# Batch 0's loads moved to another queue, and the copies of batches 0 and 1 reordered over ScalarE and VectorE

## The chip, the cores and the metric

The kernel runs on one core of one Trainium2 chip. A core has a matrix engine (TensorE, PE in the profile, its weight loads PEld), a vector engine (VectorE, DVE), an activation engine (ScalarE, ACT), GpSimd (POOL) and a queue engine (SyncE, SP). Each works through its own instructions in order, and they wait for each other by semaphores. Transfers are issued from SP's, ACT's or POOL's queue and share 16 DMA engines. The metric is device microseconds of one execution; the median of several executions is compared.

## What is computed

An efficient attention per batch and head, and a gated feed-forward block on its result, in float32 at the interfaces:

```python
# q, k, v: (8, 8, 576, 64)
q_s = softmax(q, axis=-1)            # over the 64 features
k_s = softmax(k, axis=2)             # over the 576 positions
kv = einsum('bhsd,bhse->bhde', k_s, v)
x = einsum('bhsd,bhde->bhse', q_s, kv)   # -> (4608 tokens, 512)
out = (silu(x @ w_gate) * (x @ w_val)) @ w_out   # 512 -> 1536 -> 512
```

## The kernel before, in words

**Attention.** Each batch is handled in two groups G of four heads. A load brings q, k or v of a group as a tile of 128 partitions x 1152 float32 (576 KB). ACT takes exponentials (`exp_of`, line 124: eq, ek). VectorE sums eq over the features, takes the reciprocal (`norm_sum`, lines 138 and 143: rs, rr) and multiplies (`norm_mul`, line 152: qs). TensorE transposes qs in nine 128x128 pieces into two banks of PSUM, of five and four pieces (`turn_pe`, line 166: tp), and they are copied to qt (`turn_out`, lines 111 and 113). TensorE multiplies ek with v (kv), which is scaled by one over the sum of ek into kn. Then kn times qt gives xp (`x_one`, line 221), and ACT (line 228) and VectorE (line 229) each copy one half of it into xt, the feed-forward's input. PSUM has eight banks here, handed out in program order as they come free.

**Feed-forward.** `m_unit` (line 278) does one of twelve slices m of the hidden width: four gate matmuls and four value matmuls per piece of tokens (line 289: g_ps, u_ps), a silu on ACT (line 297) and a product on VectorE into hr (line 298). Batch 0's 576 tokens are two pieces of 320 and 256. `o_mm` (line 314) makes 128 output tokens in twelve matmuls, `o_out` copies them on VectorE (line 322) and stores them from SP. `o_last` (line 328) does the final 128 tokens in two halves of 256 columns.

**Order.** The order of each engine's instructions is the order of the program text (`tc.manual_schedule`). Batch 0 comes first and is written out by hand: its q and k loads for both groups and its v loads (cast to bfloat16 on the way, v16) are POOL DMAs (lines 344 to 350), followed in POOL's queue by the making of the identity, half of one multiply (line 368) and 14 weight loads (lines 372 to 375). Its key sums come from small matmuls (`key_sum`, line 385: ks, kvr), its kv from `kv_first` (line 396) and its scaling from `scale_first` (line 409: one half on ACT, one on VectorE). `spin` (line 377) issues matmuls on zeros that nobody reads; they keep TensorE busy. Then come the twelve slices of batch 0, while SP loads batches 1 and 2. These loads wait until the second of four w_out loads has landed (line 440). Next is a stage that interleaves batch 1's attention (`kv_one`, `scale_one`) with output units 0 to 3 (lines 446 to 475), after which ACT takes batch 2's exponentials. From line 477 on, chunks of 512 tokens (the first of 448) run with the attention of the next batch between their slices.

Of the kernel before, what the change touches and what calls it, by code (L numbers as in the profile page):

```python
# [15 lines left out]
def kernel(  # L16
# [10 lines left out]
    nc = tc.nc  # L27
# [19 lines left out]
    def bank(name):  # L47
        return psp.tile([128, 512], FP32, tag="ps", name=name)
# [16 lines left out]
    def head_ap(src, b, G, t0=0, t1=T):  # L65
        return bass.AP(
            tensor=src.tensor,
            offset=src[b, 4 * G].offset + 64 * t0,
            ap=[[T * 64, 128], [2 * HSTR, 2], [1, (t1 - t0) * 64]],
        )  # L70
# [48 lines left out]
    def exp_of(what, b, G, pieces=((0, T),)):  # L119
        s = st.setdefault((b, G), {})  # L120
        e = s["e" + what] = at.tile([128, T, 2, 64], BF16, tag="e" + what, name="e" + what)
        src = raw[what, b, G].rearrange("p h (t d) -> p t h d", d=64)
        for t0, t1 in pieces:
            nc.scalar.activation(out=e[:, t0:t1], in_=src[:, t0:t1], func=AF.Exp)  # L124
# [7 lines left out]
    def norm_sum(b, G, pieces=((0, T),)):  # L132
        s = st[b, G]
        eq2 = s["eq"].rearrange("p t h d -> p (t h) d")
        rs = at.tile([128, 2 * T], FP32, tag="rs", name="rs")
        first = None
        for t0, t1 in pieces:
            i = nc.vector.reduce_sum(  # L138
                out=rs[:, 2 * t0:2 * t1], in_=eq2[:, 2 * t0:2 * t1, :], axis=mybir.AxisListType.X
            )  # L140
            first = first or i
        rr = s["rr"] = at.tile([128, 2 * T], FP32, tag="rr", name="rr")
        nc.vector.reciprocal(out=rr, in_=rs)
        return first

    def norm_mul(b, G, pieces=((0, T),), engs=None):
        s = st[b, G]
        eq2 = s["eq"].rearrange("p t h d -> p (t h) d")
        qs = s["qs"] = at.tile([128, T, 128], BF16, tag="qs", name="qs")
        for (t0, t1), eng in zip(pieces, engs or (nc.vector, nc.vector)):  # L150
            n = 2 * (t1 - t0)
            eng.tensor_mul(  # L152
                qs[:, t0:t1, :].rearrange("p t (h d) -> p (t h) d", d=64),
                eq2[:, 2 * t0:2 * t1, :],
                s["rr"][:, 2 * t0:2 * t1].to_broadcast([128, n, 64]),
            )
# [13 lines left out]
    def turn_out(b, G, i, eng):  # L170
        s = st[b, G]
        t0, t1 = BANKS[i]
        copy(
            eng,
            s["qt"][:, t0:t1, :],
            s["tp", i][:, 0:(t1 - t0) * 128].rearrange("p (t c) -> p t c", c=128),
        )
# [23 lines left out]
    def scale_one(b, G, engs):  # L201
        s = st[b, G]
        kn = s["kn"] = at.tile([128, 2, 128], BF16, tag="kn1", name="kn1")
        for g in range(2):
# [5 lines left out]
            else:  # L210
                nc.vector.tensor_scalar_mul(kn[:, g, :], kv[:, 0:128], kvr)

    def x_one(b, G):
        s = st.pop((b, G))
        for t0, t1 in BANKS:
            n = 64 * (t1 - t0)
            xp = [bank("xp") for _ in range(2)]
            for g in range(2):
                for h in range(2):
                    r = slice(64 * h, 64 * h + 64)  # L220
                    nc.tensor.matmul(  # L221
                        out=xp[h][64 * g:64 * g + 64, 0:n],
                        lhsT=s["kn"][r, g, r],
                        rhs=s["qt"][r, t0:t1, 64 * g:64 * g + 64],
                        start=True, stop=True,
                    )
            c0 = b * S + 64 * t0
            nc.scalar.copy(out=xt[:, 2 * G, c0:c0 + n], in_=xp[0][:, 0:n])  # L228
            nc.vector.tensor_copy(out=xt[:, 2 * G + 1, c0:c0 + n], in_=xp[1][:, 0:n])

# [45 lines left out]
    def m_unit(c0, n, m, by_part=False):  # L278
        ms = slice(m * 128, (m + 1) * 128)
        parts = [(c0, n)] if n <= 512 else [(c0, 320), (c0 + 320, n - 320)]  # L280
        gu = []
        for w, nm in ((wg, "g_ps"), (wv, "u_ps")):
            ps = [bank(nm) for _ in parts]
            steps = [(kk, i) for kk in range(KT) for i in range(len(parts))]
            if by_part:
                steps.sort(key=lambda a: (a[1], a[0]))
            for kk, i in steps:
                c, w_ = parts[i]
                nc.tensor.matmul(  # L289
                    out=ps[i][:, 0:w_], lhsT=w[:, kk, ms], rhs=xt[:, kk, c:c + w_],  # L290
                    start=(kk == 0), stop=(kk == KT - 1),
                )
            gu.append(ps)
        for g_ps, u_ps, (c, w_) in zip(gu[0], gu[1], parts):
            r = c % RING
            sg = ff.tile([128, 512], BF16, tag="sg", name="sg")
            nc.scalar.activation(out=sg[:, 0:w_], in_=g_ps[:, 0:w_], func=AF.Silu)  # L297
            nc.vector.tensor_mul(hr[:, m, r:r + w_], sg[:, 0:w_], u_ps[:, 0:w_])  # L298
# [18 lines left out]
            )  # L317
        return o_ps

    def o_out(j, o_ps):  # L320
        o_sb = osb.tile([128, 512], FP32, tag="o_sb", name="o_sb")
        nc.vector.tensor_copy(out=o_sb, in_=o_ps)  # L322
        store(j, o_sb)

    def o_unit(j):
        o_out(j, o_mm(j))

    def o_last(j):
        r0 = (j * 128) % RING
        o_sb = osb.tile([128, 512], FP32, tag="o_sb", name="o_sb")  # L330
        for c0 in (0, 256):
            o_ps = bank("o_ps")
            for m in range(MT):
                nc.tensor.matmul(  # L334
                    out=o_ps[:, 0:256], lhsT=hr[:, m, r0:r0 + 128], rhs=wo[:, m, c0:c0 + 256],
                    start=(m == 0), stop=(m == MT - 1),
                )
            nc.vector.tensor_copy(out=o_sb[:, c0:c0 + 256], in_=o_ps[:, 0:256])
            store(j, o_sb, c0, c0 + 256, (nc.sync, nc.scalar))

    with tc.manual_schedule():
        for what, src in (("q", q), ("k", k)):
            for G in range(NG):
                t_ = raw[what, 0, G] = ld.tile([128, 2, T * 64], FP32, tag=what, name=what)
                nc.gpsimd.dma_start(out=t_, in_=head_ap(src, 0, G))
        nc.gpsimd.dma_start(out=v16[0], in_=head_ap(v, 0, 0))
        for t0, t1 in BANKS:
            nc.gpsimd.dma_start(out=v16[1][:, :, 64 * t0:64 * t1], in_=head_ap(v, 0, 1, t0, t1))  # L350

# [6 lines left out]
            nc.vector.memset(sel[64 * g:64 * g + 64, g:g + 1], 1.0)  # L358
        for vb in vbs:
            nc.vector.memset(vb[:, :, 128:129], 1.0)  # L360
        make_identity(nc, ident)

        exp_of("q", 0, 0, BANKS)
        exp_of("q", 0, 1)
        exp_of("k", 0, 0)

        first = norm_sum(0, 0, BANKS)
        norm_mul(0, 0, BANKS, (nc.vector, nc.gpsimd))
        norm_sum(0, 1)
        norm_mul(0, 1, BANKS)  # L370

        for c0, n in ((0, 128), (128, 256), (384, 384), (768, 384), (1152, 384)):
            w_slice(wg, moe_w_gate, c0, n)
# [32 lines left out]
                        start=(t == 0), stop=(t == T - 1),  # L406
                    )

        def scale_first(G):
            s = st[0, G]  # L410
            kn = s["kn"] = at.tile([128, 2, 128], BF16, tag="kn1", name="kn1")
            nc.scalar.mul(kn[:, 0, :], s["kv"][0][:, 0:128], s["kvr"][:, 0:1])
            nc.vector.tensor_scalar_mul(kn[:, 1, :], s["kv"][1][:, 0:128], s["kvr"][:, 1:2])

        spin(8)
        spin(6, first)
        turn_pe(0, 0, 0)
        turn_pe(0, 0, 1)
        turn_out(0, 0, 0, nc.scalar)
        turn_out(0, 0, 1, nc.scalar)  # L420
        exp_of("k", 0, 1)
        key_sum(0)
        spin(3)
        turn_pe(0, 1, 0)
        turn_pe(0, 1, 1)
        turn_out(0, 1, 0, nc.scalar)
        turn_out(0, 1, 1, nc.vector)
        key_sum(1)
        spin(2)
        kv_first(0)  # L430
        scale_first(0)
        spin(2)
        x_one(0, 0)
        kv_first(1, *BANKS[0])
        kv_first(1, *BANKS[1])
        scale_first(1)
        spin(2)
        x_one(0, 1)

        load_batch(1, w_dma[-3], by_group=True)  # L440
        load_batch(2)
# [1 line left out]
        for m in range(MT):  # L443
            m_unit(0, S, m, by_part=(m == 0))

        for G in range(NG):
            exp_of("q", 1, G)
            exp_of("k", 1, G)
            cast_v(1, G)
        norm_sum(1, 0)  # L450
        norm_mul(1, 0)
        o_unit(0)
        o_unit(1)
        turn_pe(1, 0, 0)
        turn_pe(1, 0, 1)
        turn_out(1, 0, 0, nc.vector)
        turn_out(1, 0, 1, nc.vector)
        kv_one(1, 0)
        norm_sum(1, 1)
        scale_one(1, 0, (nc.vector, nc.vector))  # L460
        norm_mul(1, 1)
        p = o_mm(2)
        x_one(1, 0)
        turn_pe(1, 1, 0)
        turn_pe(1, 1, 1)
        o_out(2, p)
        turn_out(1, 1, 0, nc.vector)
        turn_out(1, 1, 1, nc.vector)
        kv_one(1, 1)
        scale_one(1, 1, (nc.vector, nc.vector))  # L470
        o_unit(3)
        x_one(1, 1)
        for what in ("q", "k"):
            for G in range(NG):
                exp_of(what, 2, G)

        chunks = [(S, 448)] + [(c, 512) for c in range(1024, n_tok, 512)]
        for ci, (c0, n) in enumerate(chunks):
# [85 lines left out]
```

## Time and profile before

| | us |
|---|---|
| median of 8 runs | 322.92 (321.64 to 324.13) |
| profiled execution, its own time | 323.65 |
| profiled execution, span from first to last instruction | 321.9 |
| TensorE busy | 310.8 (97%) |
| first gate matmul of batch 0 starts | 19.14 |
| first output matmul starts | 42.86 |
| first gate matmul of the chunk loop starts | 58.30 |
| last copy of an output starts | 317.84 |

The page gives busy time and clock by engine, and the groups of instructions. The timeline gives for each instruction or run of like instructions its start, its duration, engine, line, operation, output and inputs, and in brackets how long the engine sat idle before it and what ended that. Durations of matmuls are of pipelined instructions, so a run of them counts by its whole length. A DMA issue is listed with its queue, size and the time from issue to landing.

### The profile page before, as it was taken

The numbers are of one execution on the slowest core, as the hardware profiler recorded it, in microseconds if no ns is written. First come the engines' busy times: TensorE is split into PE (matmuls) and PEld (weight loads), VectorE is DVE, ScalarE is ACT, GpSimd is POOL, SyncE is SP. The second block draws the span as 40 slices with busy tenths as digits, with TensorE's granted clock in tenths as the row PEclk, the third lists the DMA queues.
The fourth block names the chain that finished last, engine by engine and source line by source line (L and its number), as shares of the span: only waits on it lengthen the run. The fifth ranks groups of instructions, "written<-read, shape, count | busy, mean of one in ns | idle before, by whom it ended". The sixth has DMA issues, their size and how long they took to land.

```text
span 321.9 us, 4888 instructions
## 1 busy us (share of the span) xinstructions
PE 310.8 (97%) x1897; PEld 153.3 (48%) x1897; DVE 164.9 (51%) x281; ACT 143.9 (45%) x209; POOL 34.1 (11%) x42
## 2 busy tenths in 40 slices
PE   5899998999999999999999999999999999999994
PEld 1468754455444444454444444444444444444443
DVE  2544459298493639363935484457545233333421
ACT  3663381744637454735574467346734122312200
POOL 7950011200200020002000200020000000000000
PEclk9799999999999999999999999999999999999999
DMA  6999999327653934584438533862420112020124
GB/s 191 239 202 204 229 397 390 118 39 230 249 114 67 336 130 103 71 305 169 102 69 266 210 77 72 241 259 56 82 67 0 35 32 65 0 63 4 34 67 100
DMA packets 39848, 45.75 MB, mean 142 GB/s; under 512 B 17424, under 2 KB 24080, under 8 KB 39824
## 3 DMA queue, kind: packets, MB, share of 16 engines
q1 hardware_dynamic: 31392, 37.63, 39.8%
q0 software_dynamic: 8272, 7.67, 13.2%
q8 instruction: 15, 0.25, 0.3%
q10 hardware_dynamic: 160, 0.13, 0.2%
q14 instruction: 9, 0.07, 0.1%
HBM read 37.75 MB, written 9.44 MB: 147 GB/s over the span
## 4 chain that ended last, share of the span: by engine, by line
PE 85%; DMA 6%; ACT 3%; DVE 3%; issue 1%; POOL 0%; ACTq 0%; POOLq 0%
PE g_ps L289 28%; PE u_ps L289 27%; PE o_ps L314 25%; DMA q<-in_q_dram 4%; PE kv L191 2%; DMA out_dram<-o_sb 2%; ACT eq L124 1%; DVE rs L138 1%; PE xp L259 1%; DVE qs L152 1%; PE o_ps L334 1%; PE idle L380 1%; ACT ek L124 1%; DVE hr L298 1%; PE kv L403 1%
## 5 line engine op out<-in xcount | busy, mean ns | idle before, releaser
L297 ACT ACTIVATE sg<-g_ps 128x512 bf16<-128x512 f32 (+2 forms) x120 | 64.9, 554 | 137.3 <-PE g_ps L289 131.8
L298 DVE TENSOR_TENSOR hr<-sg,u_ps 128x512 bf16<-128x512 bf16 (+2 forms) x120 | 74.4, 630 | 89.1 <-PE u_ps L289 80.4
L289 PE MATMUL g_ps<-xt,wg 128*128 128x512 bf16 (+2 forms) x480 | 111.6, 358 | 0.3 <-ACT xt L228 0.2
L289 PE MATMUL u_ps<-xt,wv 128*128 128x512 bf16 (+2 forms) x480 | 111.0, 358 | 0.0
L314 PE MATMUL o_ps<-wo,hr 128*128 128x512 bf16 x420 | 93.6, 379 | 0.0
L289 PEld LDWEIGHTS <-wv 128*128 128x128 bf16 x480 | 46.9, 98 | 46.7 <-issue 0.4
L289 PEld LDWEIGHTS <-wg 128*128 128x128 bf16 x480 | 45.8, 98 | 45.4 <-issue 1.4
L314 PEld LDWEIGHTS <-hr 128*128 128x128 bf16 x420 | 40.9, 98 | 49.1
L322 DVE COPY o_sb<-o_ps 128x512 f32<-128x512 f32 x35 | 23.7, 681 | 40.3 <-PE o_ps L314 40.3
L127 POOL CAST vb<-v 128x1152 bf16<-128x1152 f32 x14 | 16.1, 1148 | 178.0 <-DMA v<-in_v_dram 151.2
L138 DVE TENSOR_REDUCE rs<-eq 128x18 f32<-128x1152 bf16 (+2 forms) x17 | 21.6, 1277 | 14.5 <-ACT eq L124 14.5
L152 DVE TENSOR_TENSOR qs<-eq,rr 128x1152 bf16<-128x1152 bf16 (+2 forms) x17 | 21.1, 1246 | 0.2
L124 ACT ACTIVATE eq<-q 128x1152 bf16<-128x1152 f32 (+2 forms) x17 | 18.0, 1101 | 5.6 <-DMA q<-in_q_dram 5.6
L124 ACT ACTIVATE ek<-k 128x1152 bf16<-128x1152 f32 x16 | 17.9, 1157 | 0.4 <-DMA k<-in_k_dram 0.3
L297 ACT ACT_TABLE_LOAD x12 | 15.4, 1283 | 0.2
L124 ACT ACT_TABLE_LOAD x11 | 14.1, 1283 | 0.2
L380 PE MATMUL idle<-zero 128*128 128x512 bf16 x23 | 9.0, 534 | 3.8 <-DVE rs L138 2.5
L191 PE MATMUL kv<-vb,ek 64*128 64x129 bf16 x252 | 8.9, 217 | 0.2 <-DVE hr L298 0.2
L191 PEld LDWEIGHTS <-ek 64*128 64x128 bf16 x252 | 7.4, 94 | 3.0 <-ACT sg L297 2.1
L267 ACT CAST xt<-xp 128x512 bf16<-128x512 f32 x12 | 6.4, 589 | 3.8 <-PE xp L259 3.8
L268 DVE CAST xt<-xp 128x512 bf16<-128x512 f32 x12 | 7.7, 682 | 0.0
L228 ACT CAST xt<-xp 128x320 bf16<-128x320 f32 (+1 forms) x8 | 2.8, 402 | 10.6 <-PE xp L221 10.6
(48 smaller groups left out, 74.8 us busy)
## 6 DMA issues: line engine op xcount, KB each, us to landing
out_dram<-o_sb SPq DMA_DIRECT2D x70, 128.0 KB, 2.4
q<-in_q_dram SPq DMA_DIRECT2D x14, 576.0 KB, 5.1
k<-in_k_dram SPq DMA_DIRECT2D x14, 576.0 KB, 7.4
v<-in_v_dram SPq DMA_DIRECT2D x14, 576.0 KB, 9.2
wo<-in_moe_w_out_dram POOLq DMA_DIRECT2D x4, 384.0 KB, 16.2
q<-in_q_dram POOLq DMA_DIRECT2D x2, 576.0 KB, 5.5
k<-in_k_dram POOLq DMA_DIRECT2D x2, 576.0 KB, 8.0
wg<-in_moe_w_gate_dram POOLq DMA_DIRECT2D x3, 384.0 KB, 10.4
```

What stands on the lines that cost most here:

```text
L124: nc.scalar.activation(out=e[:, t0:t1], in_=src[:, t0:t1], func=AF.Exp)
L127: nc.gpsimd.tensor_copy(out=vbs[G][:, :, 0:128].rearrange("p t (h d) -> p t h d", d=64), in_=raw["v", b, G].rearrange("p h (t d) -> p t h ...
L138: i = nc.vector.reduce_sum(out=rs[:, 2 * t0:2 * t1], in_=eq2[:, 2 * t0:2 * t1, :], axis=mybir.AxisListType.X)
L152: eng.tensor_mul(qs[:, t0:t1, :].rearrange("p t (h d) -> p (t h) d", d=64), eq2[:, 2 * t0:2 * t1, :], s["rr"][:, 2 * t0:2 * t1].to_broadca ...
L191: nc.tensor.matmul(out=kv[g][:, c:c + 129], lhsT=ek_of(b, G, g, t), rhs=vbs[G][r, t, 0:129], start=(t == 0), stop=(t == T - 1),)
L268: nc.vector.tensor_copy(out=xt[:, 2 * G + 1, c0:c0 + 512], in_=main[G][1])
L289: nc.tensor.matmul(out=ps[i][:, 0:w_], lhsT=w[:, kk, ms], rhs=xt[:, kk, c:c + w_], start=(kk == 0), stop=(kk == KT - 1),)
L297: nc.scalar.activation(out=sg[:, 0:w_], in_=g_ps[:, 0:w_], func=AF.Silu)
L298: nc.vector.tensor_mul(hr[:, m, r:r + w_], sg[:, 0:w_], u_ps[:, 0:w_])
L314: nc.tensor.matmul(out=o_ps, lhsT=hr[:, m, r0:r0 + 128], rhs=wo[:, m, :], start=(m == 0), stop=(m == MT - 1),)
L322: nc.vector.tensor_copy(out=o_sb, in_=o_ps)
L380: i = nc.tensor.matmul(out=idle, lhsT=zero[:, 0:128], rhs=zero, start=True, stop=True)
```

## The change

Before batch 0's arithmetic: q and k are now issued by SP, group by group, and v by POOL with its first transfer made to wait until the second q transfer has landed; the identity is made first of all; group 1's exponentials and sums are cut in two pieces; POOL's half of the multiply goes to VectorE. In batch 0's hand-written part, `x_one` is split into its matmuls (`x_mm`) and its copies (`x_out`, with an engine per half), the steps are reordered, and there are fewer idle matmuls. In `m_unit` with `by_part`, gate and value matmuls of the first piece of tokens now precede those of the second. In batch 1's stage, copies and exponentials are reordered and some go from VectorE to ACT. The copies of `o_last` are cut in two, one for each engine.

```diff
@@ -210,23 +210,31 @@
             else:
                 nc.vector.tensor_scalar_mul(kn[:, g, :], kv[:, 0:128], kvr)
 
+    def x_mm(b, G, i):
+        s = st[b, G]
+        t0, t1 = BANKS[i]
+        xp = [bank("xp") for _ in range(2)]
+        for g in range(2):
+            for h in range(2):
+                r = slice(64 * h, 64 * h + 64)
+                nc.tensor.matmul(
+                    out=xp[h][64 * g:64 * g + 64, 0:64 * (t1 - t0)],
+                    lhsT=s["kn"][r, g, r],
+                    rhs=s["qt"][r, t0:t1, 64 * g:64 * g + 64],
+                    start=True, stop=True,
+                )
+        return xp
+
+    def x_out(b, G, i, xp, engs=(nc.scalar, nc.vector)):
+        t0, t1 = BANKS[i]
+        n = 64 * (t1 - t0)
+        c0 = b * S + 64 * t0
+        for h in (h for h in range(2) if engs[h] is not None):
+            copy(engs[h], xt[:, 2 * G + h, c0:c0 + n], xp[h][:, 0:n])
+
     def x_one(b, G):
-        s = st.pop((b, G))
-        for t0, t1 in BANKS:
-            n = 64 * (t1 - t0)
-            xp = [bank("xp") for _ in range(2)]
-            for g in range(2):
-                for h in range(2):
-                    r = slice(64 * h, 64 * h + 64)
-                    nc.tensor.matmul(
-                        out=xp[h][64 * g:64 * g + 64, 0:n],
-                        lhsT=s["kn"][r, g, r],
-                        rhs=s["qt"][r, t0:t1, 64 * g:64 * g + 64],
-                        start=True, stop=True,
-                    )
-            c0 = b * S + 64 * t0
-            nc.scalar.copy(out=xt[:, 2 * G, c0:c0 + n], in_=xp[0][:, 0:n])
-            nc.vector.tensor_copy(out=xt[:, 2 * G + 1, c0:c0 + n], in_=xp[1][:, 0:n])
+        for i in range(2):
+            x_out(b, G, i, x_mm(b, G, i))
 
 
 
@@ -279,18 +287,18 @@
         ms = slice(m * 128, (m + 1) * 128)
         parts = [(c0, n)] if n <= 512 else [(c0, 320), (c0 + 320, n - 320)]
         gu = []
-        for w, nm in ((wg, "g_ps"), (wv, "u_ps")):
+        for nm in ("g_ps", "u_ps"):
             ps = [bank(nm) for _ in parts]
-            steps = [(kk, i) for kk in range(KT) for i in range(len(parts))]
-            if by_part:
-                steps.sort(key=lambda a: (a[1], a[0]))
-            for kk, i in steps:
-                c, w_ = parts[i]
-                nc.tensor.matmul(
-                    out=ps[i][:, 0:w_], lhsT=w[:, kk, ms], rhs=xt[:, kk, c:c + w_],
-                    start=(kk == 0), stop=(kk == KT - 1),
-                )
             gu.append(ps)
+        steps = [(a, kk, i) for a in range(2) for kk in range(KT) for i in range(len(parts))]
+        if by_part:
+            steps.sort(key=lambda a: (a[2], a[0], a[1]))
+        for a, kk, i in steps:
+            c, w_ = parts[i]
+            nc.tensor.matmul(
+                out=gu[a][i][:, 0:w_], lhsT=(wg, wv)[a][:, kk, ms], rhs=xt[:, kk, c:c + w_],
+                start=(kk == 0), stop=(kk == KT - 1),
+            )
         for g_ps, u_ps, (c, w_) in zip(gu[0], gu[1], parts):
             r = c % RING
             sg = ff.tile([128, 512], BF16, tag="sg", name="sg")
@@ -317,9 +325,9 @@
             )
         return o_ps
 
-    def o_out(j, o_ps):
+    def o_out(j, o_ps, eng=nc.vector):
         o_sb = osb.tile([128, 512], FP32, tag="o_sb", name="o_sb")
-        nc.vector.tensor_copy(out=o_sb, in_=o_ps)
+        copy(eng, o_sb, o_ps)
         store(j, o_sb)
 
     def o_unit(j):
@@ -335,17 +343,19 @@
                     out=o_ps[:, 0:256], lhsT=hr[:, m, r0:r0 + 128], rhs=wo[:, m, c0:c0 + 256],
                     start=(m == 0), stop=(m == MT - 1),
                 )
-            nc.vector.tensor_copy(out=o_sb[:, c0:c0 + 256], in_=o_ps[:, 0:256])
+            nc.vector.tensor_copy(out=o_sb[:, c0:c0 + 128], in_=o_ps[:, 0:128])
+            nc.scalar.copy(out=o_sb[:, c0 + 128:c0 + 256], in_=o_ps[:, 128:256])
             store(j, o_sb, c0, c0 + 256, (nc.sync, nc.scalar))
 
 
 
+    make_identity(nc, ident)
     with tc.manual_schedule():
-        for what, src in (("q", q), ("k", k)):
-            for G in range(NG):
-                t_ = raw[what, 0, G] = ld.tile([128, 2, T * 64], FP32, tag=what, name=what)
-                nc.gpsimd.dma_start(out=t_, in_=head_ap(src, 0, G))
-        nc.gpsimd.dma_start(out=v16[0], in_=head_ap(v, 0, 0))
+        for G in range(NG):
+            qd = load("q", q, 0, G)
+            load("k", k, 0, G)
+        d = nc.gpsimd.dma_start(out=v16[0], in_=head_ap(v, 0, 0))
+        tc.add_manual_dep(d.ins, qd.ins.name, SYNC, reason="order of loads")
         for t0, t1 in BANKS:
             nc.gpsimd.dma_start(out=v16[1][:, :, 64 * t0:64 * t1], in_=head_ap(v, 0, 1, t0, t1))
 
@@ -358,16 +368,13 @@
             nc.vector.memset(sel[64 * g:64 * g + 64, g:g + 1], 1.0)
         for vb in vbs:
             nc.vector.memset(vb[:, :, 128:129], 1.0)
-        make_identity(nc, ident)
 
         exp_of("q", 0, 0, BANKS)
-        exp_of("q", 0, 1)
         exp_of("k", 0, 0)
-
+        exp_of("q", 0, 1, BANKS)
         first = norm_sum(0, 0, BANKS)
-        norm_mul(0, 0, BANKS, (nc.vector, nc.gpsimd))
-        norm_sum(0, 1)
-        norm_mul(0, 1, BANKS)
+        norm_mul(0, 0, BANKS)
+        norm_sum(0, 1, BANKS)
 
         for c0, n in ((0, 128), (128, 256), (384, 384), (768, 384), (1152, 384)):
             w_slice(wg, moe_w_gate, c0, n)
@@ -406,36 +413,42 @@
                         start=(t == 0), stop=(t == T - 1),
                     )
 
-        def scale_first(G):
+        def scale_first(G, eng1):
             s = st[0, G]
             kn = s["kn"] = at.tile([128, 2, 128], BF16, tag="kn1", name="kn1")
             nc.scalar.mul(kn[:, 0, :], s["kv"][0][:, 0:128], s["kvr"][:, 0:1])
-            nc.vector.tensor_scalar_mul(kn[:, 1, :], s["kv"][1][:, 0:128], s["kvr"][:, 1:2])
+            if eng1 is nc.scalar:
+                nc.scalar.mul(kn[:, 1, :], s["kv"][1][:, 0:128], s["kvr"][:, 1:2])
+            else:
+                nc.vector.tensor_scalar_mul(kn[:, 1, :], s["kv"][1][:, 0:128], s["kvr"][:, 1:2])
 
         spin(8)
         spin(6, first)
+        key_sum(0)
         turn_pe(0, 0, 0)
         turn_pe(0, 0, 1)
         turn_out(0, 0, 0, nc.scalar)
+        exp_of("k", 0, 1)
         turn_out(0, 0, 1, nc.scalar)
-        exp_of("k", 0, 1)
-        key_sum(0)
-        spin(3)
+        norm_mul(0, 1, BANKS)
+        spin(6)
+        key_sum(1)
+        kv_first(0)
+        scale_first(0, nc.scalar)
         turn_pe(0, 1, 0)
         turn_pe(0, 1, 1)
-        turn_out(0, 1, 0, nc.scalar)
+        turn_out(0, 1, 0, nc.vector)
         turn_out(0, 1, 1, nc.vector)
-        key_sum(1)
-        spin(2)
-        kv_first(0)
-        scale_first(0)
-        spin(2)
-        x_one(0, 0)
+        xp0 = x_mm(0, 0, 0), x_mm(0, 0, 1)
         kv_first(1, *BANKS[0])
         kv_first(1, *BANKS[1])
-        scale_first(1)
-        spin(2)
-        x_one(0, 1)
+        x_out(0, 0, 0, xp0[0], (nc.scalar, nc.scalar))
+        x_out(0, 0, 1, xp0[1], (nc.vector, None))
+        scale_first(1, nc.vector)
+        xp1 = x_mm(0, 1, 0), x_mm(0, 1, 1)
+        x_out(0, 1, 0, xp1[0], (nc.scalar, nc.vector))
+        x_out(0, 0, 1, xp0[1], (None, nc.vector))
+        x_out(0, 1, 1, xp1[1], (nc.scalar, nc.vector))
 
         load_batch(1, w_dma[-3], by_group=True)
         load_batch(2)
@@ -443,36 +456,41 @@
         for m in range(MT):
             m_unit(0, S, m, by_part=(m == 0))
 
-        for G in range(NG):
-            exp_of("q", 1, G)
-            exp_of("k", 1, G)
-            cast_v(1, G)
+        exp_of("q", 1, 0)
+        exp_of("k", 1, 0)
+        exp_of("q", 1, 1)
+        cast_v(1, 0)
+        cast_v(1, 1)
         norm_sum(1, 0)
         norm_mul(1, 0)
-        o_unit(0)
-        o_unit(1)
+        norm_sum(1, 1)
+        o_out(0, o_mm(0), nc.scalar)
+        o_out(1, o_mm(1), nc.scalar)
+        exp_of("k", 1, 1)
         turn_pe(1, 0, 0)
         turn_pe(1, 0, 1)
-        turn_out(1, 0, 0, nc.vector)
-        turn_out(1, 0, 1, nc.vector)
+        turn_out(1, 0, 0, nc.scalar)
+        turn_out(1, 0, 1, nc.scalar)
         kv_one(1, 0)
-        norm_sum(1, 1)
         scale_one(1, 0, (nc.vector, nc.vector))
         norm_mul(1, 1)
         p = o_mm(2)
         x_one(1, 0)
+        o_out(2, p)
         turn_pe(1, 1, 0)
         turn_pe(1, 1, 1)
-        o_out(2, p)
-        turn_out(1, 1, 0, nc.vector)
-        turn_out(1, 1, 1, nc.vector)
+        turn_out(1, 1, 0, nc.scalar)
+        turn_out(1, 1, 1, nc.scalar)
         kv_one(1, 1)
         scale_one(1, 1, (nc.vector, nc.vector))
-        o_unit(3)
+        p = o_mm(3)
+        exp_of("q", 2, 0)
+        exp_of("q", 2, 1)
         x_one(1, 1)
-        for what in ("q", "k"):
-            for G in range(NG):
-                exp_of(what, 2, G)
+        o_out(3, p)
+        exp_of("k", 2, 0)
+        exp_of("k", 2, 1)
+
 
         chunks = [(S, 448)] + [(c, 512) for c in range(1024, n_tok, 512)]
         for ci, (c0, n) in enumerate(chunks):
```

## The prediction

> **What bounds the kernel now.** I read the page first, then the chain of waits, the timeline of the first 30 us and of 38 to 60 us, one-microsecond windows for the granted clock, and DMA landings by issue. The page says that TensorE is the bound:
>
> ```profile
> PE 310.8 (97%) x1897; PEld 153.3 (48%) x1897; DVE 164.9 (51%) x281; ACT 143.9 (45%) x209; POOL 34.1 (11%) x42
> PEclk9799999999999999999999999999999999999999
> ```
>
> From about 60 us on the chain is matmul after matmul without a hole, so only what brings the first gate/value matmul forward, or closes a hole before 60 us, moves the end. The start is in the timeline (start, duration, engine, line, operation, then idle time and what ended it):
>
> ```profile
> 5.38 1.25 ACT L124 ACTIVATE eq<-q 128x640 bf16<-128x640 f32 x2 [3.15 <-DMA q<-in_q_dram]
> 10.26 1.35 DVE L138 TENSOR_REDUCE rs<-eq 128x18 f32<-128x1152 bf16 x1 [1.53 <-ACT eq L124]
> 12.64 1.18 ACT L124 ACTIVATE ek<-k 128x1152 bf16<-128x1152 f32 x1
> 13.43 0.40 PE L166 MATMUL tp<-ident,qs 128*128 128x128 bf16 x4
> 14.11 0.90 PE L380 MATMUL idle<-zero 128*128 128x512 bf16 x2
> 14.94 1.14 PE L403 MATMUL kv<-v,ek 64*128 64x128 bf16 x18
> 17.61 0.69 PE L403 MATMUL kv<-v,ek 64*128 64x128 bf16 x18
> 19.14 1.35 PE L289 MATMUL g_ps<-xt,wg 128*128 128x320 bf16 x8
> ```
>
> Real work starts at 19.14. VectorE waits until 10.26 for group 1's exponentials, kv of group 0 starts only at 14.94, and idle matmuls sit between its steps. Batch 1 leaves further holes:
>
> ```profile
> 48.37 0.68 PE L166 MATMUL tp<-ident,qs 128*128 128x128 bf16 x9 [0.16 <-DVE qs L152]
> 52.30 0.86 PE L221 MATMUL xp<-qt,kn 64*64 64x320 bf16 x8
> 53.99 0.68 PE L166 MATMUL tp<-ident,qs 128*128 128x128 bf16 x9 [0.83 <-DVE qs L152]
> 58.30 0.55 PE L289 MATMUL g_ps<-xt,wg 128*128 128x448 bf16 x2
> ```
>
> The transposes of group 1 wait 0.83 us for VectorE. The eight xp matmuls at 52.30 take 0.86 us against 0.44 at 57.93: 0.42 us is waiting inside.
>
> **The change, part by part.** *Loads.* Five landings (issue, size, us to landing): the first POOL load, and SP's first q and k loads at 35.8, 74.3 and 104.3 us.
>
> ```profile
> q<-in_q_dram POOLq DMA_DIRECT2D x1, 576.0 KB, 4.1
> q<-in_q_dram SPq DMA_DIRECT2D x1, 576.0 KB, 5.0
> k<-in_k_dram SPq DMA_DIRECT2D x1, 576.0 KB, 6.0
> q<-in_q_dram SPq DMA_DIRECT2D x1, 576.0 KB, 4.7
> q<-in_q_dram SPq DMA_DIRECT2D x1, 576.0 KB, 4.2
> ```
>
> SP's first load takes 4.2 to 5.0; I take 4.7, the row whose queue carried least else. SP is free at 0.8 us, each issue takes 0.5, and loads on it land in turn, 1.5 us apart (40.8 and 42.3 for the pair above). So q0, k0, q1, k1 of batch 0 land at 5.5, 7.0, 8.5 and 10.0, against 5.4, 10.5, 9.0 and 12.0 now. The first is no earlier; k gains most.
>
> POOL loses four issues (3.05 us) but gains a wait: v of group 0 waits for q1's landing, 8.5. Behind it in POOL's queue stand the other v loads and all fourteen weight loads. With the 4.1 of POOL's first load, v0 lands at 12.65 and the last piece of v at 14.15 (now 13.3 and 14.8). POOL also loses the 1.61 us multiply that held the weights until 9.58; the first weight issue comes after three v issues of 0.75, at 10.8. That is later, but the weights now land 5.9 us after issue because they queue behind q, k and v, and that backlog ends 0.65 us sooner. So I put weights 0.65 earlier, and bound it by +0.5 (an empty DMA pipe while v waits) and -1.0. Either end is covered at batch 0: the tightest, wv's third slice, lands at 22.8 (issue 13.6, 9.2 later) and is needed 6.9 us after the first real matmul, at 23.3.
>
> *Batch 0.* ACT: eq0 5.5 to 6.75, ek0 7.05 to 8.2, eq1 8.55 to 9.85. VectorE repeats its present spacing from q0 (landing 5.38, first multiply 7.90, so 2.52 later): qs0, now both halves here (0.83 + 0.69), 8.0 to 9.55; sums of group 1 (0.8 + 0.67) to 11.0; reciprocals 0.27 + 0.17; qs1 (0.83 + 0.69) ends at 12.95. TensorE: six idle matmuls 7.15 to 9.5, ks0 0.4, nine transposes to 11.0. ACT: qt0's first half (0.69) to 11.2, ek1 1.16 to 12.36. Six idle matmuls hide under ek1. ks1 ends at 12.8; kv0 (0.69) 12.8 to 13.5, v0 landing 0.15 before. Then scaling, now twice on ACT, 2 x 0.37 to 14.3, under which the transposes of group 1 (0.65) fit; xp0 0.44; kv1 0.69 to 15.5; scaling 0.4; xp1 0.44; **first real matmul 16.4**. Its operands come from ACT and VectorE copies (0.44, 0.49) ending about 0.25 us later, as the g_ps pair at 19.14 waits 0.23 today. Put at nothing: the identity, made first on POOL (0.54 us, under the 5 us in which it would wait anyway), and the four xp banks held at once. Two of them are wanted again by xp1's second half near 16.2 and are freed by ACT's two copies of xp0 (14.65 to 15.5, 0.44 each): cover 0.7 us, beyond which each 0.1 of delay costs 0.1. The same copies stand ahead of kn in ACT's queue and end just as kv1 does. The new order, value matmuls of part 0 before gate matmuls of part 1 (4 x 0.14 each), hides the rest of the copies. Gain 19.14 - 16.4 = 2.7 us.
>
> The spread around it is the clock. Rows of one microsecond (PE, PEld, DVE, ACT, POOL, granted clock, DMA share, GB/s):
>
> ```profile
> 11.00:12.00 1.00, 0.26 (x10) 0.26 (x11) 0.93 (x3) 1.00 (x2) 1.00 (x3) 1.00 1.20 204
> 13.00:14.00 1.00, 0.81 (x14) 0.46 (x12) 0.59 (x3) 1.00 (x2) 0.78 (x2) 1.00 1.67 183
> 15.00:16.00 1.00, 1.00 (x19) 0.82 (x18) 0.00 (x0) 0.00 (x0) 1.00 (x3) 0.50 1.51 186
> 18.00:19.00 1.00, 1.00 (x22) 0.38 (x16) 0.71 (x3) 0.57 (x2) 0.61 (x1) 1.00 1.31 200
> ```
>
> After a stretch with TensorE about two thirds busy, 11 to 14.3, the clock is halved until 17.6. The change cuts the idle matmuls after the first 14 from 9 to 6. [...] By the row alone, my schedule from 11 to 14.3 keeps TensorE some 85% busy, like 7.5 to 10.6, after which full clock was granted: kv costs 0.69. [...] I take full clock; the other is a rival.
>
> *Batch 1.* ACT now copies o_ps 0 and 1 (0.59 each) and both qt (0.69 + 0.59), which frees VectorE to sum group 1 before kv; its multiply then ends before xp, and both waits (0.42 + 0.83) go: 1.25 us. Added wait: in ACT's queue o_ps 0, ek1 and qt0 stand behind eq of batch 1's group 1, whose q lands at 45.8 today, 45.15 with the weights 0.65 earlier. TensorE, 2.7 earlier, enters this stage at 40.16 instead of 42.86. So eq1 ends 46.3, two copies 47.5, ek1 48.65, qt0 49.95; TensorE wants xp at 52.30 - 2.7 = 49.6: a new stall of 0.35. Gain 0.9; bounds 0.25 (loads not earlier: stall 1.0) and 1.25. Moving batch 2's k exponentials relieves ACT after it and should free the 0.16 us hole near 71.
>
> *The end.* The last copy (0.42 on VectorE) becomes two of 128 columns, 0.28 each by the 128x128 casts. Side by side that saves 0.14; one after the other it costs 0.14. The row gives no order. [...] I take +0.15.
>
> Sum: 2.7 + 0.9 + 0.15 - 0.15 = 3.6 us. The profiled execution took 323.65 (span 321.9), so 320.05; on the median, 322.92 - 3.6 = **319.3**. A difference under 0.3%, 1.0 us, can't be told from no change.
>
> **Rivals.** (B) Clock halved during batch 0, as now: 3.6 - 1.3 = 2.3, 320.6. For it: the present trace does this; against: 85% busy. 0.18. (C) Everything early, SP's first landing 4.2 and no batch 1 stall: 3.6 + 0.5 + 0.35 + 0.3 = 4.7, 318.2; 0.07. (D) The SP loads share the engines and land together near 9 instead of in turn: VectorE's chain starts 3.5 late, qs1 ends at 16.5, real work near 19.4; only batch 1 gains: 322.4. Against: loads at 35.8 landed in turn; for: POOL's q1 came 3.66 us after q0. 0.09. (E) Slower: the wait put ahead of POOL's queue. If q1's landing slips, v and every weight slip with it. Today wv's third slice lands at 22.8 and is used at 26.0, so the kernel loses once weights come more than 3.2 us later; with the DMA engines otherwise empty, that means q1 landing after 12.5. At 13.5 it is about 1 us slower: 323.9. Every SP first pair landed within 6.6 us, so 0.08.
>
> **How the numbers follow.** Forecast (318.5 to 320.4) 0.58, B 0.18, C 0.07, D 0.09, E 0.08. The range 318.2 to 321.6 holds the forecast, B and half of C. Faster: forecast, B and C, 0.83; same 0.09 (D); slower 0.08 (E).
>
> **What would show it.** First gate matmul near 16.4; q0, k0, q1, k1 in turn from about 5.5; kv0 near 12.8 on full clock, v0 landing just before; no 0.83 wait ahead of batch 1's second transposes, and a short stall at xp<-qt instead; the two last copies one after the other. Wrong if idle time on TensorE at 12 to 17 us is ended by v, if the clock row reads 0.50 there, or if wg or wv end waits of real matmuls.

## The result, and the profile after

The changed kernel takes 320.21 us in the median (319.75 to 320.78, 11 runs), the kernel before in the same comparison 322.93 (321.36 to 324.13, 32 runs): ratio 0.9918, 95% interval 0.9903 to 0.9934, 2.7 us less. The profiled execution took 320.28, its span is 318.1; beside the profile of before that is 3.4 and 3.8 us less, because that execution of before was 0.7 above its median.

TensorE is busy for 2.7 us less, and its granted clock (second row) reads 9, 90% or more, in every slice but the last:

```profile
PE 308.1 (97%) x1894; PEld 152.3 (48%) x1894; DVE 163.2 (51%) x277; ACT 147.7 (46%) x218; POOL 29.6 (9%) x37
PEclk9999999999999999999999999999999999999998
```

The timeline of the start, with the same columns as before:

```profile
4.64 1.25 ACT L124 ACTIVATE eq<-q 128x640 bf16<-128x640 f32 x2 [2.41 <-DMA q<-in_q_dram]
8.32 1.26 ACT L124 ACTIVATE eq<-q 128x640 bf16<-128x640 f32 x2 [1.06 <-DMA q<-in_q_dram]
8.60 0.86 POOL L357 DMA_DIRECT2D v<-in_v_dram  x1 [7.30 <-DMA q<-in_q_dram]
12.55 0.68 PE L410 MATMUL kv<-v,ek 64*128 64x128 bf16 x18 [0.78 <-DMA v<-in_v_dram]
15.92 0.90 PE L298 MATMUL g_ps<-xt,wg 128*128 128x320 bf16 x4
18.53 1.15 PE L298 MATMUL g_ps<-xt,wg 128*128 128x320 bf16 x8 [0.30 <-DMA wg<-in_moe_w_gate_dram]
20.59 1.15 PE L298 MATMUL u_ps<-xt,wv 128*128 128x320 bf16 x8 [0.91 <-DMA wv<-in_moe_w_val_dram]
```

The first gate matmul comes 3.2 us earlier, at 15.92 instead of 19.14. But kv waits 0.78 us for v, and the next slice of the hidden width waits 1.2 us (0.30 and 0.91) for weights, which never ended a wait of these matmuls before. The windows (columns as in the prediction) show a stretch, 8.5 to 10.2, in which almost nothing was moved:

```profile
8.50:10.20 1.70, 1.70 (x23) 1.13 (x22) 1.20 (x3) 1.70 (x4) 1.60 (x3) 1.00 0.09 27
10.20:16.00 5.80, 4.25 (x76) 2.63 (x74) 3.67 (x11) 3.45 (x9) 5.80 (x8) 1.00 1.29 156
```

The last numbers of the first row are a DMA share of 0.09 and 27 GB/s: q and k have nearly all come, v has only just been issued. Batch 1's stage:

```profile
45.70 1.16 ACT L124 ACTIVATE eq<-q 128x1152 bf16<-128x1152 f32 x1 [1.16 <-DMA q<-in_q_dram]
50.57 0.44 PE L220 MATMUL xp<-qt,kn 64*64 64x320 bf16 x8
51.16 0.68 PE L166 MATMUL tp<-ident,qs 128*128 128x128 bf16 x9 [0.15 <-DVE qs L152]
55.46 0.55 PE L298 MATMUL g_ps<-xt,wg 128*128 128x448 bf16 x2
```

The xp matmuls take 0.44 instead of 0.86 and the second transposes wait 0.15 instead of 0.83. ScalarE waits for batch 1's q, as foreseen, but that reaches TensorE with this 0.15 at most: the multiply ahead of the transposes took 1.77 us here and 1.35 before, which may be the cause as well.

Four points of TensorE's timeline divide the work, in us. "Loop" is the first gate matmul of the chunk loop, "first chunk" the first output matmul after it:

| kernel | first gate | first output | loop | first chunk |
|---|---|---|---|---|
| before, first profile | 19.14 | 42.86 | 58.30 | 84.95 |
| after, first profile | 15.92 | 41.18 | 55.46 | 81.16 |
| before_again | 16.44 | 40.16 | 55.59 | 82.24 |
| after_again | 15.56 | 40.64 | 54.87 | 80.57 |
| start_only | 15.72 | 41.30 | 56.88 | 83.53 |
| stage_only | 16.80 | 40.51 | 54.62 | 80.32 |
| exps_late | 15.78 | 41.43 | 55.47 | 82.11 |
| v_after_k0 | 15.11 | 39.08 | 53.53 | 79.23 |

In the first pair, the gain is 3.22 at the first gate matmul, 1.68 at the first output, 2.84 at the loop and 3.79 after the first chunk. From there on both run alike.

### The profile page after: what moved, and what is told of

The parts are those of the page before. It is cut to its first block, busy times and chain, and to the rows that moved or that the text cites. A ratio compares the mean times of both kernels' runs of the same rounds, so it can differ in the third digit from the quotient of the medians.

```text
span 318.1 us, 4887 instructions
## 1 busy us (share of the span) xinstructions
PE 308.1 (97%) x1894; PEld 152.3 (48%) x1894; DVE 163.2 (51%) x277; ACT 147.7 (46%) x218; POOL 29.6 (9%) x37
## 4 chain that ended last, share of the span: by engine, by line
PE 82%; DMA 12%; POOL 1%; DVE 1%; SPq 1%; ACT 1%; issue 0%
PE o_ps L322 26%; PE g_ps L298 26%; PE u_ps L298 26%; DMA q<-in_q_dram 5%; DMA wo<-in_moe_w_out_dram 5%; PE kv L191 2%; DMA wv<-in_moe_w_val_dram 2%; PE xp L267 1%; PE o_ps L342 1%; SPq L77 1%; DVE qs L152 1%; POOL wg L99 0%; POOL v L360 0%; DVE rs L138 0%; ACT eq L124 0%
## 5 line engine op out<-in xcount | busy, mean ns | idle before, releaser
L113 DVE COPY o_sb<-o_ps 128x512 f32<-128x512 f32 x33 | 22.4, 680 | 39.2 <-PE o_ps L322 39.2
L152 DVE TENSOR_TENSOR qs<-eq,rr 128x1152 bf16<-128x1152 bf16 (+2 forms) x18 | 22.1, 1239 | 0.1
L387 PE MATMUL idle<-zero 128*128 128x512 bf16 x20 | 7.8, 555 | 2.7 <-DVE rs L138 1.5
```

The costliest lines, as they stand in the source:

```text
L113: eng.tensor_copy(out=out, in_=in_)
L152: eng.tensor_mul(qs[:, t0:t1, :].rearrange("p t (h d) -> p (t h) d", d=64), eq2[:, 2 * t0:2 * t1, :], s["rr"][:, 2 * t0:2 * t1].to_broadca ...
L387: i = nc.tensor.matmul(out=idle, lhsT=zero[:, 0:128], rhs=zero, start=True, stop=True)
```

## The experiments

They ran in three groups on other chips, each beside the kernel before, which took 321.1, 321.3 and 321.4 us there, some 1.6 less than in the result's comparison. The first group is start_only, stage_only, v_after_k0 and w_slices, the second after_again, before_warm, v_no_wait and exps_late, the third the rest; runs of different groups also differ in the chip. The ratios are to the kernel before of the same group and lie within 0.2% of those of the medians; differences in us are of medians.

**start_only and stage_only** divide the change. The first is the changed kernel with the old lines from batch 1's `exp_of` to the loop and the old final copy; the second is the kernel before with the new ones, and its start untouched.

> The changed start (loads, batch 0, part order) with the old batch 1 stage and the old last copy. Theory 1 (the start gains 3.2 us at the first gate matmul and loses about 1.2 of it waiting for the second slices of wg and wv; the rest carries through): first output matmul near 41.2, 1.7 before the old 42.9, and a total some 1.0 to 1.7 us below before, 321.2 to 321.9. Rival (batch 1's loads land when they did, so the old stage gives the start's gain back): first output matmul near 41.2 but the chunk loop starts at 58 as before, total within 0.4 us of before.

Measured: 322.08, ratio 1.0020 (1.0003 to 1.0038): 1.0 us above before, and only just clear of no change. One wait stands at the same place as in the changed kernel:

```profile
19.71 1.15 PE L298 MATMUL g_ps<-xt,wg 128*128 128x320 bf16 x8 [1.67 <-DMA wg<-in_moe_w_gate_dram]
```

> The old start with the new batch 1 stage, exponential order and last copy. Theory 1 (the reordered stage is worth about 2.1 us, half of it after 58 us, where TensorE followed ScalarE and VectorE although its row reads busy): 320.8 to 321.2. Rival (the prediction's sum: 0.9 to 1.25 for the two waits, 0.15 later, minus 0.15 at the end): 321.7 to 322.0.

Measured: 318.94, ratio 0.9925 (0.9896 to 0.9954), 2.2 us less. The text of start_only expected a gain, that of stage_only had the size right (2.1): the start by itself is no gain here, and the stage is worth all of it. The table agrees, beside before_again: 1.3 us less from first output to loop, and 0.95 from there through the first chunk. The old start in stage_only reaches its first output matmul at 40.51, before the new one (41.30).

**after_again, before_again and before_warm** ask why. The first two are the two kernels unchanged. The third adds idle matmuls to the kernel before:

```diff
         exp_of("k", 0, 1)
+        spin(5)
         key_sum(0)
```

> The changed kernel itself once more, as the yardstick for the runs beside it. The first comparison gave a ratio of 0.992. Theory 2 (the old start, where the clock happens to stay full, is as fast as the new one, so the start's worth depends on how often the clock is halved in it, and the stage carries the rest): if the kernel before is near 321 here, the changed kernel is some 1 to 1.7 us below it, if near 323, 2.7 below. Rival (the start's gain is the same everywhere): 2.7 below in either case.

Measured: 319.85, ratio 0.9962 (0.9950 to 0.9974): 1.5 us less, as theory 2 has it. The changed kernel takes what it took in the first comparison; the kernel before differs.

> The kernel before itself, for a second profile. Theory 2 (most of the difference between the two yardsticks, 322.9 and 321.2, lies in the start: clock halved there or not, loads landing a little later or earlier): first gate matmul near 16.9 with the clock full from 11 to 17 us, first output matmul near 40.6, everything after that as in the first profile (14.1 to 15.5 us from the first output matmul to the chunk loop's first gate, 26.7 us from there to its first output matmul). Rival: first gate matmul near 19 again and the difference lies in a later stage.

Measured in one execution: 321.04. Its start is not the one that I had read:

```profile
7.09 1.16 ACT L124 ACTIVATE eq<-q 128x1152 bf16<-128x1152 f32 x1 [0.39 <-DMA q<-in_q_dram]
16.44 1.34 PE L289 MATMUL g_ps<-xt,wg 128*128 128x320 bf16 x8
```

```profile
11.00:14.30 3.30, 2.74 (x42) 1.59 (x41) 1.65 (x6) 2.35 (x5) 3.30 (x6) 1.00 1.52 185
14.30:17.60 3.30, 3.28 (x46) 1.71 (x45) 2.09 (x6) 2.38 (x7) 3.27 (x5) 1.00 1.42 190
```

Group 1's q lands 2.0 us earlier than in the first profile (7.09 against 9.06) and the clock is full. kv starts at 13.39 instead of 14.94, so 1.55 of the 2.70 us comes from before kv. From kv to the first gate matmul it takes 3.05 instead of 4.20, the 1.15 where the first profile has the clock at half. After that the two profiles agree to 0.01 us from first output to loop plus first chunk (42.08 and 42.09).

The mean clocks on record say how common the halved clock is there. Of the 69 executions of before beside the experiments, 11 had a mean clock of 0.989 or less (the first profile had 0.989). They took 322.2 us in the median, the other 58 took 321.3. Of the changed kernel's 17 executions on record none was under 0.997.

> The kernel before with five more idle matmuls, between the first transposes and the first key sums, where TensorE waited 1.4 us. Theory 2 (the clock was halved from 14.4 to 17.6 because TensorE was only two thirds busy from 11 to 14.3): clock full in every execution, first gate matmul near 16.8 instead of 19.1, first output matmul near 40.5, runs within 1 us of each other, total 0.5 to 2 us below before. Rival (the halving comes from elsewhere, or the idle matmuls delay the key sums): first gate matmul at 17.5 or later, total within 0.3 of before or above.

Measured: 321.40, ratio 1.0005 (0.9996 to 1.0014), first gate at 17.09, clock 0.999. It can't decide: in its group only 2 of 23 executions of the kernel before had a mean clock of 0.989 or less.

**no_spin** takes idle matmuls from the changed kernel.

```diff
         norm_mul(0, 1, BANKS)
-        spin(6)
         key_sum(1)
```

> The changed kernel without the six idle matmuls between the transposes and the second key sums. Theory 2 (idle matmuls there keep the clock): TensorE under 60% busy from 9.5 to 13, clock 0.50 for some 3.4 us after it, first gate matmul near 16.5, part of the loss covered by the wait for wg and wv; total 0.3 to 1.2 above the changed kernel's 319.9. Rival (no idle matmuls needed, and those six even delay the key sums): clock 1.00 throughout, total within 0.2 of the changed kernel.

Measured: 320.85, ratio 0.9972 (0.9951 to 0.9993), 1.0 us above after_again. The clock is what theory 2 said, for longer than it said:

```profile
12.00:13.00 1.00, 0.21 (x6) 0.20 (x7) 0.32 (x2) 0.00 (x0) 1.00 (x2) 0.50 1.30 165
19.00:20.00 1.00, 1.00 (x6) 0.54 (x5) 0.00 (x0) 0.99 (x2) 0.40 (x2) 0.50 1.27 194
```

It is half from about 10.8 to 21 us and the first gate matmul comes at 17.81. The mean clock was 0.989 or less in 8 of the 12 executions and full in the fastest (319.70). So the six idle matmuls left by the change were enough in all 17 executions of the changed kernel, and needed in most.

**v_after_k0, v_no_wait and w_slices** are about the weights. The first:

```diff
-            qd = load("q", q, 0, G)
-            load("k", k, 0, G)
+            load("q", q, 0, G)
+            kd = load("k", k, 0, G)
+            qd = kd if G == 0 else qd
```

> The changed kernel with v waiting for the first k load instead of the second q load. Theory 1 (the DMA engines stand empty from 8.5 to 10.2 because POOL waits for q1; the weights are 1.2 to 1.5 late for that reason): v and weights land 1.3 to 2 us earlier, no wait for wg or wv at slice 1, kv of group 0 no later; first output matmul near 40, total 318.7 to 319.3. Rival (the weights are slow by themselves, small pieces issued one per 0.75 us): wv's second slice still lands near 20, total 320.0 to 320.4.

Measured: 317.99, ratio 0.9887 (0.9863 to 0.9910), the best of all, 1.9 us under after_again. v is issued at 6.49, kv starts at 11.84 without a wait, and the windows where the DMA engines stood empty are full:

```profile
9.00:10.00 1.00, 1.00 (x15) 1.00 (x13) 1.00 (x2) 0.45 (x2) 1.00 (x2) 1.00 1.18 189
10.00:11.00 1.00, 1.00 (x7) 0.44 (x5) 0.95 (x4) 1.00 (x2) 1.00 (x3) 1.00 1.31 169
```

wv's second slice lands at 18.5 (issue 10.97, 7.5 later) instead of 20.5 (13.10, 7.4 later), no matmul waits for a transfer, and the first output matmul comes at 39.08, 1.56 before after_again's. Of that, 0.45 is there at the first gate matmul (15.11), since kv no longer waits for v; nearly all of the rest is the weights (waits of 0.58 and 0.43 us in after_again). The rival is out: the pieces and their order are the same.

v_no_wait only drops the wait (the `add_manual_dep` line).

> The changed kernel with v and the weights waiting for nothing. Theory 1 (the empty DMA engines were what made v and the weights late): no empty stretch, weights at least as early as with the wait on k0, no wait for wg or wv, total 317.8 to 318.8. Rival (the transfers share the engines, so q1 and k1 land 2 to 3 us later and VectorE's chain with them): first gate matmul at 17 or later, total 319 to 320.5.

Measured: 318.92, ratio 0.9942 (0.9920 to 0.9963). Both texts hold in part, and the time lies between theirs: no wait for weights, first output matmul at 40.21, but the first gate matmul slips to 16.50 and TensorE waits 1.3 us for ek1. This is 0.9 us under after_again, so the wait as built costs more than it brings. Made for one load less, as in v_after_k0, it pays.

w_slices cuts the second weight slice, `(128, 256)`, into `(128, 128), (256, 128)`.

> The changed kernel with the second weight slice of 256 columns loaded as two of 128. Theory 1 (slice 1 of the hidden width waits for a transfer twice as large as it needs): the waits for wg and wv at slice 1 (1.2 us) fall under 0.3, first output matmul near 40.2, total 319.2 to 319.8, the rest going to batch 1's q. Rival (the two more issues delay everything behind them): waits move to slice 2 or 3, total 320.2 or more.

Measured: 319.98, ratio 0.9955 (0.9939 to 0.9971), no different from after_again. The rival was right about the wait, which moved two slices on; its time, 320.2 or more, was not reached.

```profile
23.84 1.15 PE L298 MATMUL u_ps<-xt,wv 128*128 128x320 bf16 x8 [0.79 <-DMA wv<-in_moe_w_val_dram]
```

Divided, the late stream still held TensorE up, by 0.79 us at a later slice.

**pool_loads** gives the changed kernel the old loads: q, q, k, k and v on POOL, no wait.

> The changed kernel with batch 0's loads as before (all on POOL, q, q, k, k, v, no wait). Theory 1 (the new queue and its wait cost, the new order of batch 0 does not): v and weights land as in the kernel with the old start, no wait for wg or wv, first gate matmul 16 to 17, total 318.6 to 319.2, 0.7 to 1.3 under the changed kernel. Rival (the reordering of batch 0 is what costs): 319.8 or more.

Measured: 321.27, ratio 0.9986 (0.9969 to 1.0003). The rival was right here: no wait for weights, yet the first gate matmul comes at 17.28 even in its profiled execution, the fastest of its twelve (319.75 to 322.01). ScalarE takes ek0 ahead of eq1, which pays when k0 lands second; with both q first (they land 4.9 us after issue in the median, the two k behind them 6.8), eq1 stands behind a k that lands third. The first key sums wait 1.01 us for ek0, until 10.92, the second 0.59 for ek1, until 13.70; in after_again they start at 7.59 and 10.81. Order of arithmetic and order of loads go together.

**exps_late** moves two exponentials back behind batch 1's copies.

```diff
         p = o_mm(3)
-        exp_of("q", 2, 0)
-        exp_of("q", 2, 1)
         x_one(1, 1)
         o_out(3, p)
+        exp_of("q", 2, 0)
+        exp_of("q", 2, 1)
```

> The changed kernel with batch 2's two q exponentials after batch 1's last copies, where they were before. Theory 3 (about 1 us of the gain arises after 55 us, since ScalarE reaches the first silu earlier and TensorE no longer waits for free banks): first chunk, from its first gate to its first output matmul, 25.9 us instead of 25.0 (as in the kernel before, 26.0), total 0.8 to 1.0 above the changed kernel. Rival (the prediction: no more than 0.15 there): total within 0.3 of the changed kernel.

Measured: 320.97, ratio 0.9979 (0.9955 to 1.0003), 1.1 above after_again by the medians. The intervals overlap; the trace is plainer. From loop to first output matmul it takes 26.64 us, after_again 25.70, both profiles of before 26.65. And the chain of waits runs through ScalarE and VectorE again, as in before:

```profile
56.06 2.23 ACT eq L124 x2
58.28 2.10 ACT ek L124 x2
...
68.82 1.21 PE kv L191 x35
```

Theory 3 holds.

**k0_old_last** is v_after_k0 with the old final copy.

> The best version so far (v waiting for k0) with the final copies whole on VectorE, as before. By the traces the two halves run one after the other (0.29 + 0.27 with 0.03 between) against 0.42 for the whole: from the last matmul's end to the last copy's end 0.15 to 0.2 less, total 317.7 to 318.0, at the limit of what the comparison can tell. Rival (something after the copies hides it, the last stores for one): no difference in the span's tail.

Measured: 318.45, ratio 0.9888 (0.9866 to 0.9911), the same. From the start of the last matmuls to the end of the last copy it takes 3.24 us instead of 3.41, but the span ends 3.66 after that instead of 3.49. The rival was right.

## Why the prediction was right, and where it was not

The time, 320.21, lies in the range and the sign is right, but the gain is 2.7 and not 3.6, and the steps are further off than the sum. Against the profiles, from which they were made:

*Landings on SP.* Foreseen 5.5, 7.0, 8.5 and 10.0; measured 4.64, 6.1, 8.3 and 9.8 (issues at 0.74 to 2.27 plus 3.9, 4.8, 6.5 and 7.5). They land in turn, so rival D fell. The queue carried nothing else at that time, and the first load, with 3.9 us, was even quicker than its quickest later one (4.2).

*First gate matmul.* Foreseen 16.4, measured 15.92. The second key sums ended at 11.77 instead of 12.8, so kv waited for v after all, and one of the three signs of being wrong came true here ("idle time on TensorE at 12 to 17 us is ended by v"). The clock stayed full as forecast, so rival B fell, and no_spin, half from 10.8 to 21 us, shows that B was real. No run shows the 1.3 us in B's sum: with the clock at half, before took 1.15 us longer than before_again from kv to the first gate matmul, and no_spin took 1.0 us more than after_again in all. But the reason given, TensorE some 85% busy from 11 to 14.3, did not hold. It was busy for 66% (2.19 of 3.30 us), less than the 70% of before, after which the clock was halved (before, then after):

```profile
11.00:14.30 3.30, 2.32 (x31) 1.28 (x32) 2.82 (x7) 3.30 (x5) 3.08 (x5) 0.99 1.45 193
11.00:14.30 3.30, 2.19 (x47) 1.65 (x46) 2.00 (x5) 1.46 (x5) 3.30 (x5) 1.00 1.29 168
```

So this part came out right by luck. The busy share of that stretch doesn't decide by itself; what does stays open.

*Weights.* This step failed: "So I put weights 0.65 earlier, and bound it by +0.5 (an empty DMA pipe while v waits) and -1.0. Either end is covered at batch 0". They came later, and ended waits of real matmuls, a second of the signs of being wrong. v itself landed as worked out (12.5 for 12.65, its last piece 14.7 for 14.15), and the first weight issue came at 10.88 for 10.8. What failed is the inference that a shorter backlog makes up for the later issue. wv's second slice, issue and us to landing, before and then after:

```profile
11.85 0.77 POOL L99 DMA_DIRECT2D wv<-in_moe_w_val_dram  x1
wv<-in_moe_w_val_dram POOLq DMA_DIRECT2D x1, 256.0 KB, 7.1
13.10 0.77 POOL L99 DMA_DIRECT2D wv<-in_moe_w_val_dram  x1
wv<-in_moe_w_val_dram POOLq DMA_DIRECT2D x1, 256.0 KB, 7.4
```

It was issued 1.25 us later and took no less time, so it landed at 20.5 instead of 18.95; wg's landed at 18.5 instead of 17.6. The empty pipe was the right mechanism, but it lasted 1.7 us and not the 0.5 of the bound. wv's second slice is needed 3.1 to 3.4 us after the first gate matmul (before, v_after_k0), about 19.2 here, so a landing as late as before's would just have done. So 2.7 foreseen became 1.68 at the first output matmul. That is rival E's mechanism in small. On the other chips it outweighed the rest of the start (first output at 40.64 after, 40.16 before), and v_after_k0 shows the remedy, 1.9 us.

*The start of before.* I read one profile as the kernel. It was an execution with late loads and half clock, so 2.7 was measured against 19.14, and 16.44 is as real. In the result's comparison the kernel before spread over 2.8 us and the changed one over 1.0. How many of its executions there had such a start is not on record (elsewhere, 11 of 69 had so low a clock). Why its loads came late, and whether the chip itself makes a difference, stays open.

*Batch 1.* Foreseen 0.9, measured 1.16 (1.68 to 2.84), and 1.2 from the pair of second profiles (15.43 to 14.23 from first output to loop). The 1.25 of removed waits is right. The stall of 0.35 foreseen at xp did not come (0.44 there); 0.15 is left, at the second transposes.

*First chunk.* The larger mistake of reading: "From about 60 us on the chain is matmul after matmul without a hole". It is not. The chain of waits of the first profile of before, between 58.9 and 71.6 us (start, us, what):

```profile
58.89 2.23 ACT eq L124 x2
61.12 2.10 ACT ek L124 x2
63.24 1.28 ACT L297
64.53 0.55 ACT sg L297
65.11 0.62 DVE hr L298
...
71.65 1.21 PE kv L191 x35
```

Four exponentials (2.23 and 2.10 us a pair) and a table load of 1.28 us stood between batch 1 and the first silu. VectorE caught up only at 71.6, where kv waited for it, while TensorE's row from 60 to 70 read 10.00 of 10.00 busy. Short waits did not show in that row: the four matmuls begun at 64.23 held TensorE for 0.89 us, most others for 0.76. In the changed kernel the chain stays on TensorE:

```profile
66.59 0.76 PE g_ps L298 x4
67.35 0.76 PE u_ps L298 x4
68.11 1.16 PE kv L191 x36
```

I foresaw 0.15 and it is 0.95, in the first pair (26.65 to 25.70) and, put back, in exps_late. The two q exponentials ahead of `x_one` run from 52.72 to 54.95 us, while TensorE makes output unit 3 (52.40 to 55.16), at no price: ScalarE then waits 0.52 us for xp.

*The end.* Foreseen 0.15 lost, my choice between two orders of which before's rows showed neither. In the changed kernel the copies run one after the other:

```profile
314.05 0.29 DVE L346 COPY o_sb<-o_ps 128x128 f32<-128x128 f32 x1 [1.02 <-PE o_ps L342]
314.37 0.27 ACT L347 COPY o_sb<-o_ps 128x128 f32<-128x128 f32 x1 [1.04 <-DVE o_sb L346]
```

They take 0.59 instead of 0.42, but k0_old_last shows that the end doesn't follow. What absorbs the 0.17 wasn't settled.

So the sum of 3.6 met the profiles' difference (1.68 + 1.16 + 0.95 is 3.8, the spans' difference) by luck: a start too large and a stage too small cancelled. Against the medians it is 0.9 too much. The likely reason is that the start's gain hangs on which start of before one meets. stage_only says what is firm: about 2.2 us from the stage.

## What to carry to other kernels

When a load is made to wait for another one, count everything behind it in the queue, and check each consumer's due time, the first ones before the rest; aim the wait at a load that leaves the DMA engines work until the waiting one arrives, and try the kernel without the wait too. Read the chain of waits through a stage before calling it bound by the busy engine. And before a start of 20 us is taken as a yardstick, look whether its loads and its clock are the same in a second execution.

## What the runs showed of the hardware

The same POOL loads of q landed at 5.4 and 9.1 us in one execution and at 5.4 and 7.1 in another; on SP the second q landed at 7.9 to 8.3 in the changed kernel's two profiles. In no_spin TensorE did nothing from 9 to 10.8 us, and the clock was then half until 21, although TensorE was busy all of 17.6 to 21. In the first profile of before it was half in two stretches of 3.4 us each (7.4 to 10.8 and 14.3 to 17.7). In the same 11 to 14.3 us, 66% busy was followed by full clock in the changed kernel and 70% busy by half clock in before.
